# Decay attention feeding a mixture of attention experts: another written order of the same steps

## The chip, the cores and the metric

The kernel runs on one core of one Trainium2 chip. The metric is the device time of one execution in microseconds. One execution was also recorded by the hardware profiler; the rows shown below come from it. Engines carry the profile's names: PE is the matmul engine (TensorE), PEld its weight loads, DVE is VectorE, ACT is ScalarE, POOL is GpSimd, SP is SyncE, which here issues nearly all DMAs.

## The reference

Two parts. The first is a linear attention whose state decays (batch 4, 8 heads, 768 positions, 48 values per head, so 384 per position). The second is, per batch, a causal softmax attention by each of four experts of width 64, projected to 384, of which the best two per position are mixed by a gate.

```python
for t in range(S):                                    # decay attention
    cur = einsum('bhd,bhe->bhde', u * k[t], v[t])
    y[t] = einsum('bhd,bhde->bhe', r[t], state + cur)
    state = w[..., None] * state + einsum('bhd,bhe->bhde', k[t], v[t])
x = y.transpose(0, 2, 1, 3).reshape(B, S, 384)
logits = x @ w_gate                                   # mixture
topk, w = best two experts per position, softmax of their logits
for e in range(4):
    q, k, v = x @ wq[e], x @ wk[e], x @ wv[e]
    a = softmax(causal(q @ k.T / sqrt(64)))
    out += (weight of e per position) * (a @ v @ wo[e])
```

## The kernel before

The work is cut into 24 chunks of 128 positions (six per batch) and, for the mixture, into eight groups of three chunks (two per batch). A step of the first part is named by its chunk, such as `a_out,7`; one of the second by group, expert or pair of experts, and tile, such as `m_turn,7,3,5`.

First part, per chunk n: `load_chunk` and `load_vh` bring k, r and v. `a_decay` multiplies k and r by tables of powers of w (by DVE for the first three chunks, which read the tables in PSUM, by POOL for the rest, which read the copies that `table_out` makes by ACT). `a_transpose` turns k and r on PE, with ACT copies. `a_scores` (L565) are the products within the chunk, `a_mask` (L571) their masking. `a_state` (L602), `a_sum` (L613, L618) and `a_put` (L623) carry the state on. `a_out` (L582) is 32 matmuls that give the chunk's output. The part with u goes another way: `a_ku` (L522, L524, POOL) multiplies k, r and u, and `a_own` (DVE) sums that per head (L534) into eight columns of the bank in which a_out puts its 384, and multiplies v by the sums (L536). `a_add` (L586, DVE) adds that to a_out's columns. `a_xt` (L630) turns the sum on PE, with a copy by ACT (L633) and the rest by DVE in `a_xl` (L640).

Second part: `m_proj` (L670) gives queries and keys, as high and low parts (L680 and L682, or L685, L687 and a DMA). `m_values` (L705) gives values and gate logits, which DVE (L708) and ACT (L710) take out of one bank, `m_gate` the weights. `m_scores` (L753, L754) go to DVE for the maximum (L760) and ACT for the exponential (L762). `m_weigh` has DVE form factors (L768, L769) and POOL apply them (L775). `m_turn` (L783) transposes on PE and copies by ACT (L787), `m_av` (L803) multiplies by the values, with copies to high (L810, ACT) and low parts (L812, DVE), and `m_out` (L826 to L828) projects, copies (L835, ACT) and stores (L840).

All matmul outputs live in four PSUM buffers `ps` of one bank each and two `psb` of two banks each. The last av step, `m_av,7,1,3,6`, goes by thirds: matmuls of one third, high copy, then low copy and the matmuls of the next third, all in one bank. `m_out,7,2`, the last tile of the output, is made and stored in two halves.

No scheduler orders the work. `ORDER` lists 1724 words. Each advances one step to its next yield, and that emits instructions on the queue of each engine, which runs them in the order emitted. What stands behind a slash are buffer numbers for what the step takes. Semaphores between engines come from the framework: it orders accesses to the same data, and any two engines' accesses to one PSUM bank, by the order in which they are emitted.

```python
    for word in ORDER.split():
        word, _, spots[:] = word.partition("/")
        name, *args = word.split(",")
        key = (name, *(int(x) for x in args))
        if key not in under_way:
            under_way[key] = steps[name](*key[1:])
        if under_way[key] is None or next(under_way[key], done) is done:
            done.add(key)
```

Of the kernel before, what the change touches and what calls it, by code (L numbers as in the profile page):

```python
# [21 lines left out]
load_chunk,2 a_state,0/1 a_transpose,0 a_decay,1,1 a_transpose,1/2 a_transpose,1 a_sum,0 a_decay,2,0 a_ku,0/0 a_ku,0  # L22
a_own,0/30 a_sum,0/1 a_state,1/1 a_scores,0/0 a_sum,1 pad,3 a_scores,1/2 a_mask,0 a_mask,1 a_decay,2,1 a_transpose,2/1
a_put,0 load_zv,2 copy_vh,2 a_transpose,2/1 load_zv,2 a_put,1 a_out,0 a_add,0 a_state,2/0 a_ku,1/0 a_decay,3,0
make_sums,1 a_sum,1/0 a_sum,2 a_transpose,2/1 a_xt,0/2 a_out,1/3 load_chunk,4 load_qk,0/4 load_chunk,3 load_vh,3
load_o,0/5 load_chunk,5 a_ku,1 load_chunk,4 load_qk,2/0 load_qk,1/1 a_own,1/0 a_add,1 a_clear,0 a_decay,3,1 a_ku,2/0
a_sum,2/1 make_lower make_sums,0 a_ku,2 a_decay,4,0 a_decay,4,1 a_transpose,2 a_scores,2/0 a_xt,0/0 hi_qk,0 a_put,2
a_transpose,3/1 a_transpose,3/0 a_xl,0/0 a_transpose,3/3 a_xt,1/2 copy_vh,3 make_lower a_xt,1 a_transpose,3 a_mask,2
a_out,2/1 a_state,3/0 a_own,2/0 a_add,2 a_xt,2/1 a_transpose,4/3 hi_qk,2 a_xl,1 a_sum,3 lo_qk,0 a_xt,2 a_scores,3/2
hi_o,0 hi_qk,1 a_transpose,4/1 load_zv,3 a_transpose,4/0 a_transpose,4 a_xl,2 lo_qk,1 lo_qk,2 m_proj,0,0,0/1  # L30
m_proj,0,0,0/0 a_put,3 a_clear,2 a_clear,1 a_ku,3/0 a_ku,3 load_chunk,5 a_decay,5,1 a_decay,5,0 load_vh,4 load_v,1/2
load_v,0/3 load_vh,5 load_chunk,6 a_decay,6,0 a_sum,3/0 m_proj,0,1,0/3 m_proj,0,1,1/0 a_mask,3 lo_o,0 hi_v,0 load_zv,3
hi_v,1 a_own,3/20 m_proj,0,0,0 a_out,3 lo_v,0 m_proj,0,1,1/0 m_proj,0,1,1 m_proj,0,1,1 m_proj,0,1,1 a_add,3 copy_vh,4
a_scores,4/1 a_state,4/0 a_ku,4/0 load_o,1/4 load_v,2/1 a_ku,4 m_proj,0,1,0 m_proj,0,1,0 m_proj,0,1,0 m_proj,0,1,0
hi_v,2 lo_v,1 lo_v,2 load_zv,5 hi_o,1 a_sum,4 m_proj,0,0,1/2 load_zv,5 m_proj,0,0,1/1 m_proj,0,0,0/01 load_chunk,6
a_sum,4/1 a_decay,6,1 m_scores,0,0,2/1 m_values,0,0/3 m_scores,0,0,2/00 m_proj,0,0,1 m_values,0,0/0 a_mask,4 load_zv,4
# [15 lines left out]
m_proj,1,1,0 m_proj,1,1,0 m_proj,1,1,0 a_own,6/00 a_transpose,7 a_out,6 m_scores,0,3,2/52 m_proj,1,1,1 m_proj,1,1,1
m_scores,0,3,0/33 a_add,6 a_state,7/3 a_scores,7/1 m_weigh,0,2/2 a_sum,7 a_mask,7 m_scores,0,3,1 m_scores,0,3,0
m_proj,1,1,1 m_scores,0,3,2 m_weigh,0,3/3 m_proj,1,1,1 a_ku,7/0 a_ku,7 m_weigh,0,2 load_vh,8 m_proj,1,0,0/45 a_sum,7/0
m_weigh,0,3 m_scores,1,0,1/0 m_proj,1,0,1/0 m_proj,1,0,1/1 m_turn,0,2,0/3 m_turn,0,2,0/6 m_values,1,2/1 m_turn,0,2,1/2
m_turn,0,2,1/7 m_proj,1,0,1 m_scores,1,0,1/01 m_turn,0,2,2/3 m_turn,0,2,2/8 a_xt,6/0 a_xt,6/0 a_xl,6/0 m_values,1,2
# [5 lines left out]
load_zv,8 a_state,8/3 a_sum,8 a_decay,10,1 a_ku,8/0 a_sum,8/1 a_clear,6 a_ku,8 a_decay,10,0 a_scores,8/2
m_proj,1,0,1/01 m_av,0,0,0,3/1 a_state,9/0 a_mask,8 a_sum,9 m_scores,1,0,2 a_put,8 m_gate,1/111 m_weigh,1,0/0
a_transpose,9/3 a_transpose,9/0 m_av,0,0,0,3/0 m_av,0,0,0,3/0 a_transpose,9/2 a_xt,7/0 m_scores,1,1,1/0 a_transpose,9
m_av,0,1,0,3/3 m_scores,1,1,2 m_av,0,1,0,3/1 a_xt,7 a_out,8/1 m_weigh,1,0 m_av,7,1,0,3 a_own,8/0 m_av,0,1,0,3/1 a_xl,7
a_add,8 m_scores,1,2,2/1 m_turn,1,0,4/2 m_turn,1,0,4/0 m_turn,1,0,3/3 m_turn,1,0,3/4 m_scores,1,1,0 m_turn,1,0,0/0
m_turn,1,0,1/1 m_turn,1,0,2/2 m_turn,1,0,1/1 m_turn,1,0,0/3 m_out,0,2/3 m_scores,1,1,1/52 m_scores,1,2,2/00
load_chunk,11 m_out,0,2/0 a_ku,9/0 a_ku,9 load_vh,11 load_zv,11 load_vh,11 load_chunk,12 load_chunk,13 load_chunk,12
load_vh,10 load_vh,10 load_chunk,11 m_scores,1,2,1/0 a_xt,8/1 a_xt,8 a_transpose,10/0 m_scores,1,1,1 a_transpose,10/1
a_put,9 a_xl,8 a_scores,9/3 m_proj,2,0,0/1 m_scores,1,2,0/1 m_turn,1,0,5/0 m_turn,1,0,2/2 m_turn,1,0,5/5  # L70
m_proj,2,0,0/0 a_transpose,10/2 a_transpose,10 m_scores,1,2,2 m_scores,1,2,1/41 a_mask,9 a_own,9/30 m_weigh,1,1/1
m_weigh,1,1 a_sum,9/0 a_clear,8 a_ku,10/0 a_decay,11,0 a_decay,12,0 a_decay,11,1 a_out,9 a_state,10/0
m_scores,1,2,0/15 m_proj,2,0,0 a_add,9 a_sum,10 m_proj,2,1,0/1 m_turn,1,1,1/2 m_turn,1,1,1/6 m_proj,2,1,0/2
m_turn,1,1,3/3 m_scores,1,3,2/0 m_turn,1,1,4/0 m_proj,2,1,0 m_turn,1,1,4/a m_proj,2,1,0 m_proj,2,1,0 a_put,10
m_out,0,0/2 m_out,0,0/1 m_turn,1,1,3/7 m_proj,2,0,1/0 m_turn,1,1,2/1 m_scores,1,2,1 m_turn,1,1,2/9 m_turn,1,1,0/2
# [813 lines left out]
```

## Time and profile before

| | us |
|---|---|
| median of 3 runs (lowest, highest) | 371.22 (371.04, 371.96) |
| the profiled execution, its own time | 371.7 |
| its span, first to last instruction | 370.0 |
| PE busy | 337.8 |
| ACT, DVE, POOL busy | 261.1, 234.6, 195.8 |
| mean granted PE clock | 0.986 |

Busy times are the union of an engine's instructions. The number in brackets at the end of a timeline row is the idle time of the engine ahead of that row, and the instruction whose end released it. The releaser is inferred: a wait for several semaphores is put down to the one that came last, so where the engine named had been done for long, another was meant. A row with a count (x32) merges instructions that follow each other.

### The profile page before, as it was taken

How to read it: one execution, taken by the hardware profiler on the slowest of the kernel's cores; microseconds unless marked ns; L12 is line 12 of the kernel's file. 1: busy time of each engine (PE TensorE's matmuls, PEld its weight loads, DVE VectorE, ACT ScalarE, POOL GpSimd, SP SyncE). 2: the span in 40 equal slices, each digit the busy share in tenths (PEclk: the TensorE clock that was granted, in tenths of full speed). 3: DMA queues.
4: the chain of work that ended last, by engine and by line, in shares of the span. 5: the costliest groups of instructions: out<-in, count | busy, mean ns of one | idle time of the engine just before them, and what ended most of it. 6: DMA issues, size and time to landing. Idle time of an engine off the chain costs nothing.

```text
span 370.0 us, 10112 instructions
## 1 busy us (share of the span) xinstructions
PE 337.8 (91%) x3806; PEld 297.8 (81%) x3806; DVE 234.6 (63%) x648; ACT 261.1 (71%) x648; POOL 195.8 (53%) x272
## 2 busy tenths in 40 slices
...
GB/s 131 135 163 153 122 178 119 65 94 174 50 155 79 149 99 61 102 143 73 203 130 71 163 150 62 23 173 96 35 196 52 104 122 3 0 194 66 21 44 64
DMA packets 118628, 39.01 MB, mean 105 GB/s; under 512 B 111026, under 2 KB 114484, under 8 KB 118580
## 3 DMA queue, kind: packets, MB, share of 16 engines
...
q8 instruction: 30, 0.49, 0.6%
...
## 4 chain that ended last, share of the span: by engine, by line
PE 54%; DVE 10%; ACT 7%; DMA 5%; SPq 3%; issue 3%; POOL 2%; DVEq 0%; ACTq 0%; POOLq 0%
PE ps L670 8%; PE ps L783 8%; PE ps L803 8%; PE ps L582 5%; PE ps L705 4%; PE psb L753 4%; PE psb L754 4%; PE ps L546 3%; PE ps L565 2%; PE ps L602 2%; DVE tk L682 2%; PE ps L826 2%; DMA rdbuf<-in_r_dram 2%; PE ps L828 2%; PE ps L827 2%
## 5 line engine op out<-in xcount | busy, mean ns | idle before, releaser
L775 POOL TENSOR_SCALAR pr<-pr,f,gate 128x128 f32<-128x128 f32 (+5 forms) x96 | 67.5, 716 | 94.8 <-DVE f L769 41.7
L787 ACT ACTIVATE pt<-ps 128x384 f32<-128x384 f32 (+2 forms) x143 | 55.2, 419 | 33.3 <-PE ps L783 32.3
L760 DVE CUSTOM_DVE_ANT_0 pr<-psb,after 128x256 f32<-128x256 f32 (+5 forms) x96 | 58.5, 619 | 22.2 <-PE ps L783 11.5
L762 ACT ACTIVATE pr<-pr,nm 128x384 f32<-128x384 f32 (+5 forms) x96 | 63.8, 666 | 7.3 <-DVE nm L760 6.5
L783 PE MATMUL ps<-ident,pr 128*128 128x128 f32 x336 | 54.9, 278 | 2.7 <-DVE ownv L586 1.3
L753 PE MATMUL psb<-tk,tq 128*128 128x384 f32 (+2 forms) x144 | 49.5, 346 | 0.3 <-DVE nm L760 0.3
L783 PEld LDWEIGHTS ps<-ident,pr 128*128 128x128 f32 x336 | 39.0, 140 | 8.3 <-ACT pt L787 2.2
L754 PE MATMUL psb<-tk,tq 128*128 128x384 f32 (+2 forms) x144 | 42.2, 311 | 0.0
L803 PE MATMUL ps<-pt,vv 128*64 128x384 f32 (+2 forms) x322 | 40.7, 391 | 1.6 <-DVE yl L812 1.6
L571 DVE TENSOR_TENSOR rabuf<-ps,before 64x512 f32<-64x512 f32 x48 | 33.1, 689 | 6.6 <-PE ps L565 5.7
L582 PEld LDWEIGHTS ps<-zvbuf,rabuf 128*64 128x64 f32 x768 | 25.9, 141 | 14.0 <-ACT rabuf L557 4.2
L582 PE MATMUL ps<-zvbuf,rabuf 128*64 128x48 f32 x768 | 28.2, 227 | 9.7 <-DVE ownv L536 5.3
L670 PE MATMUL ps<-xt_hi,wqk_hi 128*128 128x384 f32 x96 | 33.9, 353 | 1.0 <-DVE xt_lo L640 0.4
L803 PEld LDWEIGHTS ps<-pt,vv 128*64 128x64 f32 x322 | 21.2, 137 | 16.8 <-issue 10.6
L670 PE MATMUL ps<-xt_hi,wqk_lo 128*128 128x384 f32 x96 | 32.4, 338 | 0.6 <-DVE wqk_lo L479 0.6
L522 POOL TENSOR_TENSOR ku<-kdbuf,uw 128x384 f32<-128x384 f32 x24 | 24.1, 1006 | 15.8 <-DVE ps L534 13.8
L670 PE MATMUL ps<-xt_lo,wqk_hi 128*128 128x384 f32 x96 | 32.3, 336 | 0.0
L557 ACT ACTIVATE rabuf<-ps 64x512 f32<-64x512 f32 x48 | 28.3, 590 | 4.1 <-PE ps L546 3.6
L753 PEld LDWEIGHTS psb<-tk,tq 128*128 128x128 f32 x144 | 27.3, 190 | 1.9 <-issue 0.7
L623 ACT ACTIVATE zvbuf<-z 64x384 f32<-64x384 f32 x48 | 24.9, 519 | 4.8 <-DVE z L613 4.3
L565 PE MATMUL ps<-rabuf,kt 128*64 128x64 f32 x768 | 27.0, 223 | 1.1 <-DVE ownv L586 1.1
L515 POOL TENSOR_TENSOR rdbuf<-rdbuf,tab_r 128x384 f32<-128x384 f32 x21 | 21.8, 1041 | 11.0 <-DMA rdbuf<-in_r_dram 11.0
...
## 6 DMA issues: line engine op xcount, KB each, us to landing
...
```

The source lines that it names most:

```text
L565: nc.tensor.matmul(ps[rows, i, p, :], kt[:, p, half], ra[:, par, i, p, :], start=True, stop=True)
L571: nc.vector.tensor_tensor(ra[rows, par].rearrange("s i p t -> s (i p) t"), ps[rows].rearrange("s i p t -> s (i p) t"), before[rows, None, ...
L582: nc.tensor.matmul(ps[half, 2 * p + par, :], ra[:, par, i, p, :], zv[:, par, i, p, :], start=True, stop=True)
L670: nc.tensor.matmul(ps, a[:, t, m0:m0 + P], x[:, t, :], start=i == 0, stop=i == n - 1)
L753: nc.tensor.matmul(o, tq[:, 0, q], tk[:, e, :n], start=True, stop=False)
L754: nc.tensor.matmul(o, tq[:, 1, q], tk[:, e, :n], start=False, stop=True)
L760: nc.vector.tensor_tensor_reduce(pr[:, :N], ps, after[:, S - N:], 1.0, 3e38, op0=OP.add, op1=OP.min, accum_out=nm)
L762: nc.scalar.activation(pr[:, :N], pr[:, :N], AF.Exp, bias=nm, scale=-1.0, accum_out=sums[:, e, j, 0:1])
L775: nc.gpsimd.tensor_scalar(p[:, :N], p[:, :N], f[:, i], gate[:, i, e:e + 1], op0=OP.mult, op1=OP.mult)
L783: nc.tensor.transpose(pst[:, j, :], mg[G]["p", e, j][:, i * C:(i + 1) * C], ident)
L787: nc.scalar.activation(pt[:, j0:], pst[:, j0:], AF.Copy)
L803: nc.tensor.matmul(psy[par * HD:par * HD + HD, j0 * C:j1 * C], vv[:, i % GC, e, :], mg[G]["t", e, i][:, j0:j1].rearrange("s j t -> s (j t) ...
```

## The change

The text of `ORDER` is replaced as a whole: another order of the same 1724 steps, each as often as before, with other buffer numbers. No step's code, no size and no buffer count changes. In the new text, accesses of two engines to one bank were counted as kept in order of issue when the order was laid out. Of some 400 lines these are the first and last ones of both orders and some with the steps of chunks 5, 7, 16, 17 and 21:

```diff
@@ -14,209 +14,210 @@
 PSUM = bass.MemoryType.PSUM
 
 ORDER = """
-load_vh,1 pad,6 warm_up/0 warm_up/0 make_after load_w pad,1 make_before zero,0 clear_vh,2 zero,2 zero,1 load_w pad,5
-powers/1 pad,0 pad,4 table,0/2 copy_vh,1 load_zv,1 load_zv,1 table,1/3 pad,2 powers load_vh,0 load_chunk,0 load_zv,0
-copy_vh,0 load_uw load_chunk,1 load_chunk,0 load_chunk,1 a_sum,0/0 clear_vh,1 make_ones make_ident clear_vh,0 load_uw
-table,0/0 table,1 load_zv,0 load_uw/1 table_out,1 table_out,0 load_uw a_decay,0,0 a_decay,1,0 a_decay,0,1
-a_transpose,1/2 a_transpose,0/3 a_transpose,1/0 a_transpose,0/1 a_transpose,0/0 load_chunk,2 load_chunk,3 load_vh,2
...
-m_scores,0,1,0/54 a_mask,5 m_weigh,0,0/0 m_scores,0,1,0 a_clear,3 load_vh,7 m_weigh,0,0 a_own,5/10 a_out,5 a_add,5
...
-a_transpose,8/1 m_scores,1,1,0/0 a_transpose,8/2 m_scores,1,1,0/23 a_own,7/00 m_gate,1 a_transpose,8 m_scores,1,0,0
-m_turn,0,3,2/b a_out,7 m_scores,1,1,2/34 a_add,7 load_vh,9 load_zv,9 load_vh,9 load_vh,8 load_chunk,10 load_zv,8
...
-m_turn,3,3,1/6 m_turn,3,3,0/a m_scores,4,0,2/21 a_xt,16 m_scores,4,1,1/1 m_turn,3,3,4/1 m_turn,3,3,4/8 a_out,17/0
-a_state,18/1 m_scores,4,1,0/0 a_transpose,18 m_turn,3,3,5/2 a_own,17/0 a_add,17 a_xl,16 a_xt,17/0 m_scores,4,1,2
...
-m_scores,7,3,1/50 m_scores,7,3,0/02 m_out,6,0/1 m_scores,7,3,2 m_turn,7,2,0/3 m_turn,7,2,4/2 m_turn,7,2,4/9 m_out,6,0
-m_out,6,2/0 m_av,7,0,0,3/2 m_scores,7,3,1 m_scores,7,3,0 m_weigh,7,3/3 m_weigh,7,3 m_turn,7,1,4/2 m_out,6,2/1
-m_turn,7,2,0/3 m_out,6,2 m_out,6,1 m_turn,7,2,5/1 m_turn,7,2,5/1 m_turn,7,2,1/0 m_turn,7,2,3/3 m_turn,7,2,2/1
-m_av,7,0,3,6 m_turn,7,2,2/a m_turn,7,2,1/0 m_turn,7,2,3/8 m_turn,7,3,1/1 m_turn,7,3,0/0 m_turn,7,3,2/3 m_turn,7,3,1/4
-m_turn,7,3,0/b m_turn,7,3,2/2 m_turn,7,3,3/1 m_turn,7,3,3/5 m_av,7,1,3,6/0 m_turn,7,3,4/3 m_turn,7,3,5/1
-m_turn,7,3,4/6 m_av,7,1,3,6/0 m_av,7,0,3,6/1 m_turn,7,3,5/0 m_av,7,1,3,6/0 m_av,7,1,3,6 m_av,7,1,3,6 m_av,7,0,3,6/1
-m_av,7,1,3,6 m_out,7,0/3 m_out,7,0/1 m_out,7,0 a_sum,11 m_av,7,1,3,6 m_out,7,2/1 m_out,7,2/0 m_out,7,2/2 m_out,7,2/0
-m_out,7,2 m_out,7,1/0 m_out,7,1/0 m_out,7,1 a_sum,5
+load_w clear_vh,1 make_ident clear_vh,0 load_w make_ones make_after zero,1 zero,2 zero,0 a_sum,0/0 make_sums,0
+load_vh,1 pad,4 pad,3 pad,1 pad,5 pad,6 pad,0 warm_up/0 warm_up/0 load_uw load_uw load_uw/1 load_chunk,0 load_vh,0
+load_zv,1 load_zv,1 copy_vh,1 load_uw copy_vh,0 load_zv,0 load_chunk,1 load_chunk,0 powers/1 powers pad,2 table,0/2
+table,1/3 table,0/0 table,1 a_decay,0,0 a_decay,1,0 a_state,0/2 a_transpose,0/3 a_decay,0,1 a_sum,0 load_chunk,1
+a_decay,1,1 a_transpose,1/0 load_zv,0 table_out,0 a_transpose,0/0 a_transpose,1/1 a_ku,0/0 a_ku,0 load_chunk,2
+load_qk,1/4 load_chunk,2 load_vh,2 a_transpose,0/1 load_chunk,3 a_transpose,0 a_sum,0/1 make_before clear_vh,2
...
+m_scores,0,1,1/55 a_transpose,6/2 a_own,5/30 a_transpose,6/0 m_scores,0,2,2/1 a_transpose,6/0 m_scores,0,2,0/0
+m_turn,0,0,0/2 a_out,5 a_sum,6 m_scores,0,2,0/03 a_add,5 load_chunk,8 a_ku,6/0 a_decay,8,0 a_sum,6/1 a_ku,6
...
+m_av,3,0,3,6/0 a_own,16/10 a_out,16 m_weigh,3,3/3 a_sum,17 m_weigh,3,3 m_proj,4,0,0/45 m_av,3,0,3,6/0 a_sum,18
...
+a_put,18 m_scores,4,1,2 m_scores,4,1,1/32 m_weigh,4,0/0 a_xl,16 m_gate,4/000 m_av,3,1,0,3/3 a_out,17/1 m_av,3,1,3,6
+a_scores,18/2 m_scores,4,1,1 a_transpose,19/1 m_av,3,1,3,6/1 a_own,17/0 m_weigh,4,0 m_weigh,4,1/1 a_add,17
...
+a_own,21/00 a_out,21 m_weigh,5,1/1 m_proj,6,1,0 m_av,4,1,0,3/3 m_proj,6,1,0 a_add,21 m_proj,6,1,1 m_proj,6,1,0
...
+m_turn,7,2,5/0 m_turn,7,2,5/4 m_turn,7,2,3/1 m_turn,7,2,1/2 m_turn,7,2,0/0 m_turn,7,2,0/9 m_turn,7,2,1/3
+m_turn,7,2,3/7 m_weigh,7,3/3 m_weigh,7,3 m_av,7,0,3,6 m_av,7,0,3,6/0 m_av,7,0,3,6/1 m_turn,7,3,0/0 m_turn,7,3,1/2
+m_turn,7,2,2/1 m_turn,7,3,0/6 m_turn,7,3,1/8 m_turn,7,2,2/0 m_turn,7,3,2/0 m_turn,7,3,2/1 m_turn,7,3,3/3
+m_turn,7,3,3/5 m_av,7,1,3,6/2 m_turn,7,2,4/1 m_turn,7,3,4/0 m_turn,7,3,5/3 m_av,7,1,3,6/1 m_turn,7,3,5/0
+m_turn,7,2,4/a m_turn,7,3,4/2 m_av,7,1,3,6/0 m_out,7,0/3 m_av,7,1,3,6 m_av,7,1,3,6 m_out,7,0/0 m_av,7,1,3,6 m_out,7,0
+m_out,7,1/1 m_out,7,1/1 m_out,7,1 m_av,7,1,3,6 m_out,7,2/0 m_out,7,2/0 m_out,7,2/3 m_out,7,2/0 m_out,7,2
 """
 
 BUFS = {
```

More of the change, by code (lines that the diff above doesn't have):

```diff
@@ L22 @@
[L22 to L36, printed above, removed]
@@ L52 @@
[L52 to L56, printed above, removed]
@@ L62 @@
[L62 to L75, printed above, removed]
-m_turn,1,1,0/8 m_values,2,0/3 m_scores,1,3,1/1 m_scores,1,3,2/33 m_scores,1,3,1/22 m_values,2,0/0 m_values,2,0/2
@@ new lines @@
+m_proj,1,0,0/0 m_scores,0,2,0 load_vh,7 load_chunk,7 load_chunk,8 load_zv,6 load_zv,6 load_zv,7 load_chunk,9 load_vh,7
+a_own,6/10 m_weigh,0,1 m_turn,0,1,0/3 m_turn,0,1,0/3 a_out,6 m_weigh,0,2/2 a_clear,4 a_decay,7,1 a_decay,8,1
+m_proj,1,0,0 a_clear,6 a_ku,7/0 a_ku,7 a_decay,9,0 m_weigh,0,2 a_state,7/0 load_vh,8 load_zv,7 load_vh,9
+m_proj,1,0,0/45 a_transpose,7/3 m_proj,1,1,1/1 m_proj,1,1,1 m_scores,0,3,0/32 m_proj,1,1,1 m_scores,0,3,0
+a_transpose,7 a_add,6 m_scores,0,3,1/1 m_proj,1,1,0/1 a_sum,7 m_proj,1,1,0 m_proj,1,1,1 m_values,1,2/0 m_values,1,2
@@ new lines @@
+a_put,8 a_mask,8 m_turn,0,3,2/3 a_xt,7/2 a_transpose,9/1 m_turn,0,3,2/b a_transpose,9/1 m_scores,1,1,0/1
+m_scores,1,0,1 a_transpose,9/3 m_av,0,1,0,3/0 a_transpose,9 m_av,0,1,0,3/1 a_xt,7 a_own,8/10 m_scores,1,1,1/45
+m_scores,1,1,0/54 m_av,0,1,0,3/1 m_weigh,1,0/0 a_out,8 a_add,8 a_xl,7 a_scores,9/3 a_state,9/0 a_sum,8/1 a_sum,9
+a_mask,9 m_scores,1,1,1 m_scores,1,1,0 a_ku,9/0 load_chunk,12 load_zv,10 load_chunk,13 load_vh,10 load_vh,10
+load_chunk,11 m_weigh,1,1/1 m_out,0,1/1 m_values,2,1/2 m_out,0,1/0 m_values,2,1/0 a_decay,10,0 m_weigh,1,0 a_xt,8/0
@@ new lines @@
+m_proj,2,1,0/2 m_scores,1,2,2 m_out,0,0/0 a_own,9/00 a_state,10/2 a_out,9 m_scores,1,3,1/43 m_proj,2,1,0
+m_scores,1,3,0/52 a_add,9 a_sum,10 a_scores,10/3 m_scores,1,3,1 m_gate,2 m_proj,2,1,0 m_proj,2,1,0 m_scores,1,3,0
+a_put,10 a_mask,10 a_scores,11/0 a_mask,11 m_proj,2,1,1/2 m_proj,2,1,1 m_proj,2,1,1 a_decay,12,0 a_decay,13,0 a_xt,9/1
+a_xt,9/1 a_decay,12,1 a_ku,10/0 a_ku,10 a_sum,10/1 a_sum,12/0 a_transpose,12/3 a_transpose,12/0 m_proj,2,0,0/23
+load_zv,12 load_vh,12 m_av,1,0,0,3/0 m_scores,1,3,2 a_xl,9/1 m_weigh,1,2/2 m_weigh,1,2 a_own,10/30 m_weigh,1,3/3
@@ new lines @@
+m_weigh,1,3 m_av,1,0,3,6 a_state,11/1 a_sum,11 m_av,1,0,3,6/0 m_proj,2,1,1 a_out,10 load_chunk,13 load_vh,12
+m_proj,2,0,1/45 m_out,0,0 m_out,0,2 a_ku,11/0 a_ku,11 m_proj,2,1,1 a_put,11 a_add,10 m_av,1,0,3,6/0 a_state,12/1
+a_sum,12 load_vh,13 load_chunk,14 load_vh,13 load_zv,12 m_turn,1,2,5/2 m_turn,1,2,5/5 m_turn,1,2,3/3 m_scores,2,0,0/1
+m_turn,1,2,3/9 m_turn,1,2,1/0 m_turn,1,2,4/2 m_turn,1,2,4/0 m_turn,1,3,5/1 m_turn,1,2,1/6 m_turn,1,3,5/1
+m_scores,2,0,2/0 m_turn,1,2,2/3 m_turn,1,2,2/4 m_turn,1,2,0/2 m_turn,1,2,0/3 m_turn,1,3,0/0 m_turn,1,3,3/1
@@ new lines @@
+a_add,11 a_xl,10 a_decay,14,0 a_clear,9 a_decay,13,1 a_ku,12/0 m_weigh,2,0 a_scores,12/2 m_turn,2,0,0/3 a_xt,11/0
+m_scores,2,2,2/1 m_turn,2,0,0/3 a_xt,11 m_out,1,0/1 m_turn,2,0,1/3 m_turn,2,0,1/8 m_scores,2,1,2 m_out,1,0/0
+m_scores,2,1,1 a_ku,12 a_clear,11 a_sum,13/0 a_clear,10 a_mask,12 a_xl,11 m_scores,2,1,0/34 m_scores,2,1,0
+a_transpose,13/2 m_proj,3,0,0/0 m_proj,3,1,0/3 m_proj,3,0,0/1 a_transpose,13 m_scores,2,2,2/20 a_own,12/10
+m_proj,3,1,0/0 m_scores,2,3,2/0 m_scores,2,2,0/1 a_out,12 m_proj,3,0,0 m_weigh,2,1/1 m_proj,3,1,0 m_proj,3,1,0
@@ new lines @@
+m_proj,3,1,1 m_scores,2,3,1/1 a_state,14/0 a_sum,14 m_scores,2,2,2 m_scores,2,2,0 m_scores,2,2,1 a_out,13
+a_scores,14/0 m_proj,3,1,1 a_add,13 m_proj,3,0,1 a_mask,14 a_put,14 m_out,1,2/2 a_decay,15,0 a_decay,16,0
+m_values,3,0/1 a_transpose,15/3 m_turn,2,1,2/0 m_weigh,2,2/2 m_values,3,0/1 m_out,1,2/1 m_values,3,0/0
+m_scores,2,3,0/0 a_transpose,15/1 m_turn,2,1,2/4 m_values,3,2/2 a_ku,14/0 load_chunk,16 a_decay,16,1 a_decay,15,1
+a_clear,13 a_transpose,16/1 a_transpose,16/0 load_chunk,18 m_proj,3,0,0/01 load_vh,16 load_vh,15 load_zv,15 load_vh,16
@@ new lines @@
+m_scores,3,1,2 m_scores,3,1,1/55 m_values,4,2/3 m_turn,3,0,1/2 m_turn,3,0,0/6 m_proj,4,1,0 m_values,4,2/0
+m_scores,3,1,0/33 m_scores,3,1,1 m_values,4,2/1 m_av,7,1,0,3 m_scores,3,1,0 a_scores,15/1 a_scores,16/0 m_av,2,1,0,3/3
+a_mask,15 m_turn,3,0,1/7 m_av,2,1,0,3/1 m_weigh,3,1/1 a_mask,16 m_av,2,1,0,3/1 load_zv,15 m_proj,3,0,1/23 load_zv,16
+load_chunk,17 a_ku,15/0 a_ku,15 a_decay,18,0 m_weigh,3,1 load_chunk,18 a_decay,18,1 a_sum,16/1 m_out,1,2 load_vh,17
+a_out,15/1 a_own,15/0 a_add,15 a_ku,16/0 a_decay,17,1 m_turn,3,0,5/2 m_out,2,2/0 m_turn,3,1,2/3 m_scores,3,2,0/0
```

301 lines of the change are left out of this document (151 added, 150 removed).

## The prediction

> **What bounds the kernel now.** I read the page first, then the waits of the matmul engine, then single places in the timeline. The profiled execution took 371.7 us for a span of 370.0 us; the median of the runs is 371.22 us, 0.48 us less. From the page (engine totals, then the chain that ended last):
>
> ```profile
> span 370.0 us, 10112 instructions
> ...
> PE 337.8 (91%) x3806; PEld 297.8 (81%) x3806; DVE 234.6 (63%) x648; ACT 261.1 (71%) x648; POOL 195.8 (53%) x272
> ...
> PE 54%; DVE 10%; ACT 7%; DMA 5%; SPq 3%; issue 3%; POOL 2%; DVEq 0%; ACTq 0%; POOLq 0%
> ```
>
> PE is busy for 337.8 of 370.0 us, so 32.2 us are idle. No other engine is above 71%. A new order adds and removes no instruction, so what it can change is these 32.2 us, plus stretches at a lower clock. Who ends PE's idle time (waits of PE: us in total, times, longest), and how long ScalarE waits for PE in one step:
>
> ```profile
> PE ps L582 <- DVE ownv L536: 5.3, 6, 2.0
> PE ps L630 <- DVE ownv L586: 2.8, 3, 1.3
> PE ps L582 <- ACT tk L680: 1.8, 2, 1.0
> PE ps L582 <- ACT rabuf L557: 1.7, 2, 1.5
> PE ps L546 <- DVE ownv L586: 1.6, 2, 1.3
> PE ps L803 <- DVE yl L812: 1.6, 2, 0.9
> PE ps L783 <- DVE ownv L586: 1.3, 1, 1.3
> PE ps L565 <- DVE ownv L586: 1.1, 1, 1.1
> PE ps L582 <- ACT pt L787: 0.3, 1, 0.3
> ...
> ACT pt L787 <- PE ps L783: 32.3, 34, 3.2
> ```
>
> The four L582 rows make 5.3 + 1.8 + 1.7 + 0.3 = 9.1 us. L582 is a_out. It needs nothing that a_own (L534, L536) computes: the two touch different columns of one bank, and only a_add (L586) needs both. Two of these waits in the timeline, chunks 5 and 7:
>
> ```profile
> 60.60 0.56 DVE L536 TENSOR_TENSOR ownv<-vhbuf,ps 128x384 f32<-128x384 f32 x1
> 61.30 1.95 PE L582 MATMUL ps<-zvbuf,rabuf 128*64 128x48 f32 x32 [2.02 <-DVE ownv L536]
> ...
> 88.25 0.55 DVE L536 TENSOR_TENSOR ownv<-vhbuf,ps 128x384 f32<-128x384 f32 x1
> 88.91 1.14 PE L582 MATMUL ps<-zvbuf,rabuf 128*64 128x48 f32 x32 [1.55 <-ACT rabuf L557]
> ```
>
> a_own ends at 61.16 and 88.80, PE starts 0.14 and 0.11 us later. So the second wait too is for a_own, though a long finished ScalarE copy is named. One bank is kept in the order of the written list, whichever columns are meant.
>
> The rest of the waits on L586 is the reverse case, a_own written behind a_out (chunk 17):
>
> ```profile
> 225.69 1.14 PE L582 MATMUL ps<-zvbuf,rabuf 128*64 128x48 f32 x32
> ...
> 226.97 0.56 DVE L534 TENSOR_REDUCE ps<-ku 128x8 f32<-128x384 f32 x1 [1.39 <-PE ps L582]
> 227.57 0.55 DVE L536 TENSOR_TENSOR ownv<-vhbuf,ps 128x384 f32<-128x384 f32 x1
> 228.16 0.56 DVE L586 TENSOR_TENSOR ownv<-ps,ownv 128x384 f32<-128x384 f32 x1
> ...
> 228.77 0.55 PE L630 MATMUL ps<-ident,ownv 128*128 128x128 f32 x3 [0.76 <-DVE ownv L586]
> ```
>
> From the end of a_out (226.83) to the next matmul that needs its sum or its bank are 1.94 us, all on VectorE. What PE has to do meanwhile is what the order decides.
>
> **The change, term by term.** Durations of PE steps, from the chain of waits (start, us):
>
> ```profile
> 75.09 1.14 PE ps L582 x32
> 76.23 0.68 PE ps L602 x16
> 76.91 0.93 PE ps L565 x32
> 78.62 1.55 PE ps L670 x9
> ...
> 113.02 0.66 PE ps L783 x6
> ```
>
> (1) a_own ahead of a_out. In the order before, 12 chunks (3, 5, 6, 7, 9, 11, 13, 14, 15, 16, 21, 23) have no PE step written between the two; PE waited in all but chunk 21, 9.1 / 11 = 0.83 us each. In the new order there are 6 such chunks (4, 8, 14, 16, 19, 21). What remains: if VectorE begins a_own as PE begins the step ahead, PE waits for 1.25 us (1.11 of a_own and 0.14) less that step. Those steps take 1.05, 0.64, 0.47, 0.68, 0.47 and 1.55 us (by the durations above; scores and value products in proportion to their columns), which leaves 0.2 + 0.6 + 0.8 + 0.6 + 0.8 + 0 = 3.0 us. The same sum over the twelve of before gives 6.5 us, where 9.1 were measured, so I raise it by 9.1 / 6.5 to 4.1 us. Gain 5.0 us. Ends: 2.5 us if all six cost 0.83 and four chunks with only 0.33 to 0.55 us between (3, 6, 7, 12) cost 0.4 each; 9.1 us if none waits.
>
> (2) a_own behind a_out: 7 chunks in both orders. PE work from the end of a_out to the next step that needs the sum or the bank, summed with the durations above: before 1.37, 0.68, 1.56, 1.32, 0.92, 0.93, 1.32 us (chunks 1, 2, 8, 10, 17, 18, 20), against the 1.94 short by 5.5 in all. New: 2.38, 1.56, 1.95, 2.13, 1.57, 3.21, 2.32 (chunks 1, 2, 15, 17, 20, 22, 23), short by 0.8. The rows on L586 hold 2.8 + 1.6 + 1.3 + 1.1 = 6.8 us, part of it where VectorE was late for other reasons. I take 4.0 us (2.0 to 6.0).
>
> (3) The end. Per third of the last output, the next matmuls into the bank wait for the copies of the third before:
>
> ```profile
> 359.34 1.31 PE L803 MATMUL ps<-pt,vv 128*64 128x128 f32 x20 [0.86 <-DVE yl L812]
> 361.38 1.42 PE L803 MATMUL ps<-pt,vv 128*64 128x128 f32 x21 [0.73 <-DVE yl L812]
> ...
> 366.57 0.49 ACT L835 ACTIVATE o<-ps 128x384 f32<-128x384 f32 x1 [1.40 <-PE ps L828]
> ...
> 367.09 0.33 SPq L840 DMA_DIRECT2D out_dram<-o  x1
> ```
>
> Ahead of the first of these waits three transposes stand as cover (3 x 0.11 us), ahead of the second nothing. New: five transposes (0.55 us) and m_out,7,0, six matmuls at 1.55 / 9 = 0.17 us, 1.03 us. So the first wait falls by 0.22 us and the second goes: 1.0 us (0.2 to 1.6). The last output is now a half, not a whole, so the copy of 0.49 us gets shorter; the store behind it stays about 2.6 us (367.42 to 370.0).
>
> (4) The start. The first decay reads the bank of tables behind ScalarE's two copies of it:
>
> ```profile
> 7.04 1.10 PE L434 MATMUL psb<-ident,pr 128*128 128x128 f32 x8 [1.21 <-DVE pr L428]
> ...
> 8.76 0.47 ACT L438 ACTIVATE tab_r<-psb 128x384 f32<-128x384 f32 x1
> 9.13 0.47 ACT L438 ACTIVATE tab_k<-psb 128x384 f32<-128x384 f32 x1
> ...
> 9.63 1.02 DVE L513 TENSOR_TENSOR kdbuf<-kdbuf,psb 128x384 f32<-128x384 f32 x2 [2.04 <-ACT tab_k L438]
> ```
>
> In the new list the decays of chunks 0 and 1 are written ahead of both copies, so they could start at 8.2, not 9.6. Against that, the loads of the rows w and u, which followed the first load of k, now go ahead of it. I take 1.0 us (-0.5 to 1.4; negative if the loads of the first chunks, issued in another order, come later).
>
> (5) The clock. Windows (us, PE, weight loads, DVE, ACT, POOL busy, then the granted clock):
>
> ```profile
> 57.50:61.00 3.50, 1.33 (x9) 1.06 (x9) 3.33 (x10) 2.74 (x6) 1.72 (x4) 1.00 0.97 183
> 61.00:64.50 3.50, 3.20 (x49) 3.01 (x49) 1.18 (x3) 1.33 (x5) 1.94 (x4) 0.51 0.69 119
> ```
>
> A stretch with PE busy for 1.33 of 3.5 us, holding two of the stalls above (a_out of chunk 5 among them), is followed by one at 0.51: 3.2 us of matmuls at half speed, 1.6 us lost. In the new order chunk 5 has 1.24 us of PE work between a_own and a_out. I take half, 0.8 us (-1.6 to 1.6), as the fall can come at another place. The Trainium skill ("TensorE: Matmul & The Clock Gate", What's actually happening) has the clock fall after at least one idle window of some 3.4 us. By that alone 2.02 us of idle would not have cost the clock and nothing would be won or lost here, and the forecast would be 0.8 x 0.7 = 0.6 us higher; the trace shows that a part-busy stretch suffices, and decides.
>
> Sum: 5.0 + 4.0 + 1.0 + 1.0 + 0.8 = 11.8 us. Not all arrives: PE comes sooner to steps whose inputs come from others. In the chain 10 + 7 + 5 + 3 + 3 + 2 = 30% of the span is not PE's, so as an estimate 30% of the gain, 3.5 us, turns into waits for loads, VectorE or GpSimd. That leaves 8.3: 371.7 - 8.3 = 363.4 us in the profile's terms, less 0.48 for the median: **362.9 us**. The ends of the terms, with the same 30%, are 2.9 us (2.5 + 2.0 + 0.2 - 0.5 and the clock as now, 4.2) and 13.8 us (9.1 + 6.0 + 1.6 + 1.4 + 1.6, 19.7). That most of it arrives is supported by the ScalarE row, 32.3 us of waiting for PE's transposes: the engines behind PE have room.
>
> **Rivals.**
> - *All of it arrives.* Nothing is given back: 371.2 - 11.8 = 359.4 us. For it: ScalarE and VectorE wait for PE. Against: the 30%.
> - *The a_out waits stay.* 17 chunks still have a_own ahead of a_out, as before. If the wait follows from that and not from the place, term 1 is nothing: (11.8 - 5.0) x 0.7 = 4.8, so 366.4 us. Against: no stall in the five chunks that had PE work between.
> - *The clock falls more often.* Two more stretches like 61.0 to 64.5, and the old one kept: 362.9 + 0.8 + 3.2 = 366.9 us.
> - *Slower: VectorE blocked by GpSimd.* Now that a_out waits for a_own in the plan, a_own is written early, and behind it on VectorE queue score reductions, masks and sums, which free PE's banks. If it comes before a_ku is done, all of them wait for a GpSimd operation:
>
> ```profile
> POOL ku L522 <- DVE ps L534: 13.8, 8, 3.9
> ...
> L524 POOL TENSOR_TENSOR ku<-ku,rdbuf 128x384 f32<-128x384 f32 x24 | 24.6, 1025 | 0.8
> ```
>
> Half of one such operation in each of 24 chunks is 24 x 0.51 = 12.3 us: 375 us. It decides from 8.3 / 24 = 0.35 us a chunk. Against it: now GpSimd waits for VectorE (13.8 us), and only 4 chunks of the new order (3 before) have under 1.5 us of PE work between a_ku and a_own.
> - *No change.* The semaphores kept each bank in order before too; the new list meets other waits of the same size, 371 us.
>
> **How the numbers follow.** Forecast 0.40, all arrives 0.20, a_out waits stay 0.17, clock 0.08, blocked by GpSimd 0.09, no change 0.06. A measurement of this kernel can tell about 0.3% (1.1 us) from nothing. Faster: 0.40 + 0.20 + 0.17 + 0.08 = 0.85; same 0.06; slower 0.09. The range takes the first four: 357.0 (371.2 less the 13.8 of the best ends is 357.4) to 369.0 us (371.2 less the 2.9 of the worst ends is 368.3). The forecast's own range is 360 to 366.
>
> **What would show it.** In the profile after: the four a_out rows fall from 9.1 to about 4 us, those on L586 from 6.8 to under 3, L803 behind L812 from 1.6 to about 0.6, VectorE's wait for tab_k is gone, and there is no stretch near 0.5 after the first 20 us. PE's idle falls from 32 to about 24 us at the same busy time. Wrong if PE's idle stays above 30 us: then look at who ends it, loads and a_ku first.

## The result, and the profile after

The kernel after takes 345.37 us (345.03 to 346.38, four runs) against 371.13 us of the kernel before on the same chip: a ratio of 0.931 [0.928, 0.935], 25.8 us faster. Measured again later, it took 344.77 against 371.84 us, 0.929 [0.926, 0.933]. The forecast was 362.9 us, range 357.0 to 369.0: the sign was right, the gain three times as large as said.

The page of the kernel after, engine totals and the chain that ended last (its lines are numbered one higher than before: a_out is L583, a_own L535 and L537, a_add L587):

```profile
span 344.7 us, 10135 instructions
...
PE 332.6 (97%) x3806; PEld 297.4 (86%) x3806; DVE 232.8 (68%) x648; ACT 261.2 (76%) x648; POOL 194.8 (57%) x272
...
PE 83%; POOL 6%; DVE 4%; ACT 4%; issue 3%; POOLq 0%; ACTq 0%; DVEq 0%
```

PE's idle time is 344.7 - 332.6 = 12.1 us, where it was 32.2. PE has 83% of the chain (77% in another execution of the same kernel, e14 below) instead of 54%. The busy times of VectorE, ScalarE and GpSimd change by less than 2 us. Who still ends idle time of PE (us in total, times, longest):

```profile
PE ps L360 <- DVE pr L356: 2.1, 1, 2.1
PE ps L804 <- DVE rabuf L572: 1.7, 2, 1.5
PE ps L671 <- DVE wqk_lo L480: 1.1, 1, 1.1
...
PE ps L583 <- ACT xt_hi L634: 0.8, 1, 0.8
...
PE ps L583 <- DVE ownv L537: 0.2, 1, 0.2
```

The a_out rows, 9.1 us before, are 0.8 + 0.2 = 1.0 us. The 0.8 us is chunk 2, whose a_own stands behind its a_out; its wait before (0.5 us, for other causes) was not among the 9.1. So of the 9.1 us 0.2 are left, those of chunk 5. There is no row for the sum of a_add (6.8 us before) and none for the last thirds behind the low copy (1.6 us before). Chunks 6 and 8 in the timeline, to be held against those of chunks 5 and 7 before:

```profile
64.24 0.56 DVE L537 TENSOR_TENSOR ownv<-vhbuf,ps 128x384 f32<-128x384 f32 x1
65.22 1.14 PE L583 MATMUL ps<-zvbuf,rabuf 128*64 128x48 f32 x32
...
88.00 0.54 DVE L535 TENSOR_REDUCE ps<-ku 128x8 f32<-128x384 f32 x1
...
88.58 0.55 DVE L537 TENSOR_TENSOR ownv<-vhbuf,ps 128x384 f32<-128x384 f32 x1
...
89.48 1.09 PE L583 MATMUL ps<-zvbuf,rabuf 128*64 128x48 f32 x32
```

The multiply is the last operation of a_own. It ends 0.42 and 0.35 us ahead of a_out, and neither a_out row has a wait. Windows of the kernel after around the place where the clock fell before (us, PE, weight loads, DVE, ACT, POOL busy, granted clock):

```profile
57.00:61.00 4.00, 3.85 (x77) 3.39 (x78) 2.81 (x11) 3.58 (x8) 3.78 (x5) 1.00 0.69 117
61.00:64.00 3.00, 3.00 (x29) 2.93 (x26) 2.44 (x6) 2.38 (x9) 2.89 (x6) 1.00 0.56 100
```

PE is busy 3.85 of 4 us where it was busy for 1.33 of 3.5, and the clock stays at 1.00. (A 128x128 transpose is issued every 0.11 us there, as at full clock elsewhere, so the column can be trusted here; see the last section.)

Idle time alone does not add up to the gain: it fell by 20.1 us, the span by 25.3. The other 5.2 us are busy time that went. The stretch at half clock was 1.6 us of it. The rest is the end of the pipeline. All 768 matmuls of a_out in the kernel after, by their line (ns: shortest, median, longest):

```profile
L583 PE MATMUL ps<-zvbuf,rabuf x768: 206/222/258, 19.4 to 286.6; 128*64 128x48 f32 x192
```

One takes 222 ns, but in the row at 65.22 us 32 of them take 1.14 us, 36 ns each, because the next starts while the last is in the pipe. When nothing follows, the last 0.222 - 0.036 = 0.19 us of the matmul, its drain, still count as busy in the profile, though no new work begins. The starts of the matmuls show what the busy time hides. Take as the usual step the median distance from a matmul of one shape to the start of the next; a start that comes more than 0.25 us later than that is a stop. Before there are 44 stops with 34.4 us of lateness together, after 17 with 10.0 us. That is 24.4 us, the gain but for the clock, and 27 stops fewer are 27 x 0.19 = 5.1 us of drains. With the clock's 1.6 us this makes 6.7 us, more than the 5.2 us of busy time that went: in the profiled execution two early steps of PE took 1.97 and 1.64 us, where the kernel before took 1.10 and 0.91 us, which is 1.6 us the other way.

### The profile page after: what moved, and what is told of

Same layout as the page of the kernel before. It is cut to its first block, busy times and chain, and to the rows that moved or that the text cites. A ratio compares the mean times of both kernels' runs of the same rounds, so it can differ in the third digit from the quotient of the medians.

```text
span 344.7 us, 10135 instructions
## 1 busy us (share of the span) xinstructions
PE 332.6 (97%) x3806; PEld 297.4 (86%) x3806; DVE 232.8 (68%) x648; ACT 261.2 (76%) x648; POOL 194.8 (57%) x272
## 4 chain that ended last, share of the span: by engine, by line
PE 83%; POOL 6%; DVE 4%; ACT 4%; issue 3%; POOLq 0%; ACTq 0%; DVEq 0%
PE ps L784 11%; PE ps L804 11%; PE ps L671 10%; PE ps L706 8%; PE psb L755 6%; PE psb L754 6%; PE ps L547 6%; PE ps L583 6%; PE ps L566 5%; PE ps L603 5%; PE ps L827 3%; PE ps L829 2%; PE ps L828 2%; PE ps L631 2%; DVE rabuf L572 2%
## 5 line engine op out<-in xcount | busy, mean ns | idle before, releaser
L763 ACT ACTIVATE pr<-pr,nm 128x128 f32<-128x128 f32 (+5 forms) x96 | 63.9, 667 | 2.4 <-DVE nm L761 1.4
L784 PE MATMUL ps<-ident,pr 128*128 128x128 f32 x336 | 52.6, 276 | 0.1
L804 PE MATMUL ps<-pt,vv 128*64 128x384 f32 (+2 forms) x322 | 40.2, 392 | 1.7 <-DVE rabuf L572 1.7
L804 PEld LDWEIGHTS ps<-pt,vv 128*64 128x64 f32 x322 | 20.9, 137 | 18.1 <-issue 12.6
L671 PE MATMUL ps<-xt_lo,wqk_hi 128*128 128x384 f32 x96 | 32.2, 336 | 0.0
L754 PEld LDWEIGHTS psb<-tk,tq 128*128 128x128 f32 x144 | 27.3, 189 | 0.8 <-DVE nm L761 0.2
L583 PEld LDWEIGHTS ps<-zvbuf,rabuf 128*64 128x64 f32 x768 | 24.8, 138 | 3.5 <-issue 1.2
L583 PE MATMUL ps<-zvbuf,rabuf 128*64 128x48 f32 x768 | 26.8, 223 | 0.9 <-ACT xt_hi L634 0.8
L755 PEld LDWEIGHTS psb<-tk,tq 128*128 128x128 f32 x144 | 27.3, 190 | 0.0
L516 POOL TENSOR_TENSOR kdbuf<-kdbuf,tab_k 128x384 f32<-128x384 f32 x21 | 21.8, 1046 | 8.3 <-DMA kdbuf<-in_k_dram 7.4
```

The costliest lines, as they stand in the source:

```text
L583: nc.tensor.matmul(ps[half, 2 * p + par, :], ra[:, par, i, p, :], zv[:, par, i, p, :], start=True, stop=True)
L671: nc.tensor.matmul(ps, a[:, t, m0:m0 + P], x[:, t, :], start=i == 0, stop=i == n - 1)
L754: nc.tensor.matmul(o, tq[:, 0, q], tk[:, e, :n], start=True, stop=False)
L755: nc.tensor.matmul(o, tq[:, 1, q], tk[:, e, :n], start=False, stop=True)
L763: nc.scalar.activation(pr[:, :N], pr[:, :N], AF.Exp, bias=nm, scale=-1.0, accum_out=sums[:, e, j, 0:1])
L784: nc.tensor.transpose(pst[:, j, :], mg[G]["p", e, j][:, i * C:(i + 1) * C], ident)
```

## The experiments

Theory A, as the first expectations call it: the gain is that of the waits which come from one bank being kept in order (a_own and a_out above all). Theory B: those waits only uncover others, and the gain is the layout as a whole.

### Is it the shared bank?

e1 is the kernel before with the eight sums of a_own in a tile of SBUF instead of in the bank of a_out. No word of the order moves.

```diff
+    ownsum = const.tile([P, H], F32, name="ownsum")
     def a_own(n):
-        own = outs(n)[:, DM:DM + H, None]
+        outs(n)
+        own = ownsum[:, :, None]
```

> The order before, but a_own puts its eight sums of every chunk into an SBUF tile, so a_own and a_out share no PSUM bank and neither waits for the other; no word of the order is moved. Theory A (the gain is the waits that come from one bank being kept in order, and all of it arrives): 9.1 us on a_out and some 5.5 of the 6.8 us on a_add go, with them about 0.17 us of matmul drain at each of some 20 stalls (3 us) and the clock's fall at 61 us (1.6 us): 371 - 19 = 352 us. Theory B (the new layout is better as a whole; a wait that goes uncovers another, as in the prediction's 30% or more): 371 - 7 to 9 = 362 to 364 us.

Measured 358.08 against 372.04 us, 0.964 [0.961, 0.967]: 14.0 us, between the two theories. The a_out rows of PE's waits in e1 (L585 there):

```profile
PE ps L585 <- ACT kt L555: 0.9, 2, 0.7
PE ps L585 <- DVE yl L815: 0.6, 1, 0.6
PE ps L585 <- DVE rabuf L574: 0.3, 1, 0.3
```

None of these is for a_own. 0.5 us of the 1.8 are chunk 2's, which stood before too, so the 9.1 us became 1.3. The waits for the sum of a_add fell as well, from 6.8 to 3.0 us: where a_own is written behind a_out, it no longer waits for a_out to end. So 14.0 of the 25.8 us that the new order gains can be had, without moving a word, from the bank that a_own and a_out share.

e2 and e3 do the same for chunks 7, 11, 14 and for chunk 5 alone (`if n in (7, 11, 14): own = ownsum[:, :, None]`).

> The order before with the sums in SBUF for chunks 7, 11 and 14 only. Their a_out waited 1.55 + 1.53 + 0.90 = 3.98 us. Theory A: these and three drains of 0.17 us arrive whole, 4.5 us, 366.6 us. Theory B: at most 70% of 3.98, 2.8 us, 368.3 us or more.

> The order before with the sums in SBUF for chunk 5 only, whose a_out waited 2.02 us just ahead of the fall of the clock at 61 us. If the clock falls because of that stall: 2.0 + 0.2 + 1.6 = 3.8 us, 367.3 us, and the profile has no half-speed stretch after 20 us. If the stall alone counts: 2.2 us, 368.9 us, with the stretch still there.

e2: 369.58 us, 0.994 [0.992, 0.997], 2.5 us (1.3 to 3.0 by the interval) of the 4.0 that it could give. e3: 369.08 us, 0.993 [0.991, 0.995], 3.0 us (1.8 to 3.5), between its two cases. The windows of its profiled execution:

```profile
57.00:60.50 3.50, 2.21 (x28) 1.97 (x29) 3.33 (x11) 2.54 (x6) 1.67 (x5) 0.89 0.90 171
60.50:64.00 3.50, 3.50 (x45) 3.28 (x42) 2.38 (x5) 1.54 (x5) 2.87 (x5) 0.62 0.70 113
```

With the stall of chunk 5 gone PE is still busy for only 2.21 of 3.5 us there, and the clock still falls (0.62). But that is one execution. The mean granted clock of a whole execution is 0.999 or 1.000 in four of the seven of e3, which as far as the clock column tells leaves no room for such a stretch (3.4 us at half clock make it 0.995); the kernel before never has more than 0.995, here and in the later experiments. So the stall of chunk 5 had a part in the fall, and is not all of it. In e1, where the neighbouring stalls go too, 57 to 64 us run at 1.00.

e4 is the same edit in the kernel after.

> The new order with the sums of every chunk in SBUF. Its waits of PE behind a_own are 0.2 us by the profile (0.8 more under another name). Theories A and B both: 0 to 1.2 us faster, 344.2 to 345.4 us. If the new order gained nothing from where a_own stands, it would gain here what the order before gains in the first of these runs.

347.7 us, 0.936 [0.932, 0.940] of the kernel before: nothing gained, and some 2 us lost, though this interval overlaps that of the kernel after. In the new order the bank costs nothing that this experiment can see. The loss may be a side cost of the SBUF tile, which e1 would pay too (last section).

### Is it the place of a_own?

e7 is the kernel after with a_own of chunks 3 to 14 moved down to stand directly ahead of their a_out. For chunk 8 (words of `ORDER`, line breaks left out):

```diff
-a_own,8/10 m_scores,1,1,1/45 m_scores,1,1,0/54 m_av,0,1,0,3/1 m_weigh,1,0/0 a_out,8
+m_scores,1,1,1/45 m_scores,1,1,0/54 m_av,0,1,0,3/1 m_weigh,1,0/0 a_own,8/10 a_out,8
```

> The new order with the a_own words of chunks 3 to 14 moved down to just ahead of their a_out, as twelve chunks of the order before had it; nothing else moves. If the place of a_own ahead of a_out decides: seven of these lose 0.5 to 1 us of cover and PE waits about 0.8 us and a drain of 0.2 at each, 349 to 352 us, with rows of a_out behind a_own of 4 to 7 us. If the new layout absorbs it: 346 to 347 us.

359.48 us, 0.966 [0.959, 0.972] of the kernel before: 13 to 14 us of the 25.8 lost again by twelve words. Seven of the twelve a_out wait again (chunks 3, 4, 5, 8, 10, 13 and 14), 10.9 us in all, where 0.2 us were left. Chunk 8 in the timeline of e7:

```profile
90.03 0.81 DVE L761 CUSTOM_DVE_ANT_0 pr<-psb,after 128x640 f32<-128x640 f32 x1
90.16 1.52 PE L804 MATMUL ps<-pt,vv 128*64 128x384 f32 x12 [1.45 <-DVE rabuf L572]
90.77 0.68 DVE L761 CUSTOM_DVE_ANT_0 pr<-psb,after 128x512 f32<-128x512 f32 x1
...
92.24 0.56 DVE L813 TENSOR_TENSOR yl<-ps,yh 128x384 fp32r<-128x384 f32 x1 [0.79 <-ACT yh L811]
...
92.99 0.53 DVE L535 TENSOR_REDUCE ps<-ku 128x8 f32<-128x384 f32 x1
93.56 0.55 DVE L537 TENSOR_TENSOR ownv<-vhbuf,ps 128x384 f32<-128x384 f32 x1
94.21 1.14 PE L583 MATMUL ps<-zvbuf,rabuf 128*64 128x48 f32 x32 [2.54 <-ACT pr L763]
```

Chunk 8 is the clearest case, because a_own moved past no PE step: the PE step ahead of a_out (L804) is written ahead of both places of a_own. What changed is VectorE's queue: a_own now stands behind two score maxima, the low copy, which itself waits 0.79 us for ScalarE, and two small operations of m_weigh. In the kernel after a_own begins at 88.00 (shown above), ahead of all of them. PE stands 2.54 us for it (the ScalarE operation named had nothing to do with a_out). Here the price of a_own's place is set by what stands ahead of it on VectorE, at the same PE work. In other chunks of e7 words of PE were passed too, and the two are not separated.

e13 asks whether the place of a_own also holds the rest: a_own early in the order before, free of the bank, on top of e5 (below).

> As e5 (the order before, sums of a_own outside the bank, copies of one bank spaced, the new end; 354.9 us), and a_own of 17 chunks written earlier, to up to 3 us of PE work ahead of a_out where a_ku and the chunk before allow it. Theory 1, the place of a_own holds the rest too (a_add and what needs its sum no longer wait for a_own): 348 to 351 us, and the waits of PE for ownv (2.5 us in e5) gone. Theory 2, the rest is spread over the places of other steps: 353.5 to 355 us. If VectorE is blocked behind GpSimd's a_ku (the rival of the prediction): 357 us or more.

358.0 us, 0.964 [0.961, 0.967], 3 us longer than e5: theory 1 fell, and the time is that of the third case. Waits of PE and of VectorE in e13:

```profile
PE ps L632 <- DVE ownv L588: 2.7, 2, 2.2
...
DVE ownsum L536 <- POOL ku L524: 1.9, 1, 1.9
```

PE now waits longer for the sum of a_add, not less (1.4 us in e5), and once VectorE stands 1.9 us for GpSimd's a_ku: the rival "blocked by GpSimd", on a small scale. The longest wait has another cause, which the rows of VectorE and GpSimd ahead of it show:

```profile
283.71 1.00 POOL L522 TENSOR_TENSOR ku<-kdbuf,uw 128x384 f32<-128x384 f32 x1
283.72 1.06 DVE L723 TENSOR_TENSOR eq<-lg 128x48 f32<-128x48 f32 x1
...
284.79 1.00 POOL L524 TENSOR_TENSOR ku<-ku,rdbuf 128x384 f32<-128x384 f32 x1
284.81 1.04 DVE L724 TENSOR_TENSOR eq<-eq,lower 128x48 f32<-128x48 f32 x1
...
285.89 0.21 DVE L725 TENSOR_TENSOR gt<-gt,eq 128x48 f32<-128x48 f32 x1
```

In e5 this a_ku waited 1.35 us for a_own and began behind these gate operations. In e13 it meets them: two that run beside it take 1.06 and 1.04 us, the next, beside no a_ku, takes 0.21. (In e5 one of the two took 0.88 us, beside another operation of GpSimd.) a_add stands behind them.

### The other pairs on one bank, and the end

Several kinds of steps let ScalarE and VectorE read one bank in turn. e6 is the kernel before with two of them relieved: m_proj's two high copies first, then both low ones, and the gate logits read by ScalarE, which reads the values too. e5 is e1 with these and with the last words in the new order's sequence.

```diff
+            for e, own in ((2 * pr, top), (2 * pr + 1, bot)):
+                nc.scalar.activation(tk[own, e, :], ps[own], AF.Copy)
             for e, own, other in ((2 * pr, top, bot), (2 * pr + 1, bot, top)):
+                yield
                 if e % 2:
                     yield
-                nc.scalar.activation(tk[own, e, :], ps[own], AF.Copy)
-                yield
...
-        nc.vector.tensor_copy(logits_of(G)[:, j, :], ps[:, NV:])
+        nc.scalar.activation(logits_of(G)[:, j, :], ps[:, NV:], AF.Copy)
```

> The order before with only the two changes to m_proj (high key parts first) and m_values (logits by ScalarE); the sums stay in PSUM, the end as it was. ScalarE waited 7.9 us for VectorE's low key parts and 7.6 us behind VectorE's copy of the logits. Theory A: PE gets a good part of it, 364 to 367 us against 372. Theory B: PE does not notice, 370 to 372 us.

> The order before with the sums in SBUF (358.1 us alone), and two more one-bank pairs eased: m_proj has ScalarE make both high key parts before VectorE makes the low ones (one change of engine per key tile instead of three), m_values takes the gate logits by ScalarE (no VectorE read of that bank); and the last words as in the new order (m_out,7,0 and m_out,7,1 between the thirds of the last av step). The end alone: 0.86 + 0.73 and two drains, 1.9 us. Theory A (what is left of the gain, 12 us, are the other pairs of engines on one bank): 358.1 - 1.9 - 6 to 9 = 347 to 350 us. Theory B (what is left belongs to the layout as a whole): 354 to 356 us.

e6: 369.52 us, 0.993 [0.990, 0.995], 2.2 us. e5: 354.87 us, 0.955 [0.951, 0.958], 16.8 us, about 3 more than e1; 1.0 of them is the end (the last 200 matmuls begin 27.9 us ahead of the end of the span instead of 28.9; 27.1 in the kernel after). By the count of late starts e5 has 28 stops with 18.7 us, the kernel after 17 with 10.0 us: the 8.7 us between are about the 9 us between their times. They are not one place: transposes of k and r 2.7 against 1.7 us, of scores 3.6 against 0.5, a_out 2.9 against 1.2, a_xt 1.8 against 0.3, m_proj 2.0 against 1.2.

e8 was to price the spaced copies in the new order by putting them back to back.

> The new order with the four words of each key projection's copies, and the two of each value product's, written directly one behind the other, as most of them are in the order before. Theory A (spread pairs are a part of the gain): ScalarE's waits for VectorE on tk and vv rise from 3.6 and 2.6 us to about 8 each, and the time by 3 to 8 us, 349 to 354 us. Theory B: no more than 1 us, 345 to 347 us.

386.13 us, 1.038 [1.035, 1.042]. Moved so, a copy of group 7 overwrites a buffer of values before `m_av,5,1,0,3` has read it, so the end of this kernel computes something else than the reference, and its time prices nothing exactly. But that copy begins at 326 us at the earliest, and a_out of chunk 23 already starts at 320.9 us, 35 us later than in the kernel after (285.7). ScalarE's waits for VectorE's copy of the logits rise from 2.6 to 17.3 us, for the low key parts from 3.6 to 9.9. So the tight copies cost far more than the 3 to 8 us of theory A. How much of it is the spacing, and how much other work that stands behind copies written earlier, is not separated.

### The start

e12 is the kernel before with the two table copies written behind the first decays; e10 and e11 are the kernel after with a longer warm-up of PE.

Part of a line of `ORDER`:

```diff
-table,1 load_zv,0 load_uw/1 table_out,1 table_out,0 load_uw a_decay,0,0 a_decay,1,0 a_decay,0,1
+table,1 load_zv,0 load_uw/1 load_uw a_decay,0,0 a_decay,1,0 a_decay,0,1 table_out,1 table_out,0
```

> The kernel before, with only the two copies of the tables by ScalarE written behind the decays of chunks 0 and 1 instead of ahead of them. If these copies are what held the first decay (as the prediction's step 4 said), it starts at 8.3 instead of 9.6 us and 1.0 to 1.3 us arrive: about 370 us. If the clock then also stays at full through the first transposes, up to 3 us more. Rival: the loads or the other copies of ScalarE are next, nothing arrives: 371.2 us.

> The kernel after, with the warm-up matmuls 1 us earlier and 15 instead of 10 of them (first word of the list; they write a bank that is not used before 40 us). In the kernel after, transposes take 213 ns each from 8.1 us to 14.4 us and 109 ns afterwards, although the page shows 1.00 for all of it. If that is half clock because the ten warm-up matmuls began only at 2.1 us, the transposes of the tables take 0.9 us instead of 2.0, the first decay starts at 9.1 instead of 10.1, and 1 us arrives at the end: 344.4 us. Rival: the first chunks are bound by the loads and by the copies of ScalarE (which released the first state step at 10.7 us): no change, 345.4 us.

> As the one before, and six more warm-up matmuls behind the transposes of the tables, where PE is idle until 10.7 us. If the clock is kept at full from there on, what ran at half until 14.4 us (about 5.5 us of PE work between 10.7 and 15.7) takes half the time, and up to 2.7 us more arrive: 342 us; transposes of 109 ns from 8 us on. If the first chunks are bound by other engines, 344 to 345.4 us.

e12: 370.05 us, 0.996 [0.993, 0.999], about 1.5 us (0.6 to 2.7 by the interval). In its profiled execution the tables' transposes took 1.94 us instead of 1.10, and the decay began at 9.02 and not at 8.3 us. e10: 344.9 us, e11: 346.5 us, both within the intervals of the kernel after. In e11 the early work came sooner and PE then stood 2.2 us at one place for a mask of VectorE (1.5 us in the kernel after). Then e10's kernel again (e15) beside the kernel after itself (e14):

> The kernel after, unchanged, to stand beside the next one: 345.4 us.

> The kernel after with 15 warm-up matmuls from 1.25 us on, beside the kernel after in the same call. The profiles differ by 1.5 us in the span (343.2 against 344.7), the medians by 0.5 us. Theory: the transposes of the tables at full clock bring the first decay 0.6 us forward and that arrives: 344.8 us. Rival: no difference.

344.77 (e14) and 344.72 us (e15): no difference, so no version here beats the kernel after. The profile of e14, the same kernel as after, tells why. The tables' transposes and the first decay in the execution shown above, then in e14:

```profile
8.08 1.97 PE L435 MATMUL psb<-ident,pr 128*128 128x128 f32 x8
10.08 1.02 DVE L514 TENSOR_TENSOR kdbuf<-kdbuf,psb 128x384 f32<-128x384 f32 x2 [2.67 <-PE psb L435]
```

```profile
6.95 1.19 PE L435 MATMUL psb<-ident,pr 128*128 128x128 f32 x8 [0.19 <-DVE pr L429]
8.18 1.19 DVE L514 TENSOR_TENSOR kdbuf<-kdbuf,psb 128x384 f32<-128x384 f32 x2 [0.75 <-PE psb L435]
```

Eight transposes take 1.97 us in one execution and 1.19 in the other; the decay starts at 10.08 or 8.18 us, the span is 344.7 or 342.6 us. When full speed comes in the first 15 us differs between executions of one kernel, and the longer warm-up bought nothing in the median.

## Why the prediction was wrong, step by step

**What bounds it** held: PE's idle time was what a new order could change. That PE's busy time would stay was wrong by 5.2 us. A wait row leaves out the 0.19 us in which the last matmul drains: 5.1 us for the 27 stops that went, which no term of the sum had. In the profile's terms the forecast was 8.3 us, terms (1) to (5), 11.8, less 3.5 given back. Measured were 25.3 us: 8.9 on a_out, 6.8 on a_add, 1.6 at the end, 2.8 of PE's other waits and 5.2 of busy time.

**(1) a_own ahead of a_out**: forecast 5.0 of 9.1 us, measured 8.9. e1 shows the cause (the shared bank), so the mechanism was right and the size was off. The failed step is "if VectorE begins a_own as PE begins the step ahead": I let a_own begin 0.47 to 1.55 us ahead of a_out, the length of the PE step ahead. In all six chunks (4, 8, 14, 16, 19, 21) a_own began 1.5 to 2.0 us ahead of a_out and ended 0.35 to 0.86 us ahead of it, so none waits. The new list writes a_own ahead of other VectorE work there, and e7 shows for chunk 8 that this place decides. For chunk 8 the length was wrong too: its PE step (L804) was put at 0.64 us and takes 1.35 us to the start of a_out. That all six would go was the term's best end, and nothing in the prediction told it from the middle.

**(2) a_own behind a_out**: forecast 4.0, measured 6.8, all of the rows on a_add. The PE work counted behind a_out was enough. The allowance for "VectorE was late for other reasons" had a ground, as 3.0 us of these rows stay in e1, where a_own waits for no a_out; but the new order lifted those too, and which words did it is not shown.

**(3) The end**: forecast 1.0, measured 1.6 by the rows (1.8 by the last 200 matmuls). The first wait, of which I left 0.86 - 0.22 = 0.64 us, went too.

**(4) The start**: the forecast "could start at 8.2" was met to 0.02 us in e14 (8.18), and e12 gained about 1.5 us by this edit alone. In the profiled execution of the kernel after, transposes at half clock (1.97 us) put it off to 10.08.

**(5) The clock**: forecast 0.8, the half of 1.6 as a guess between its ends; measured 1.6, the half stretch is gone. The stall of chunk 5 was a part of the reason and not all of it: with it taken away (e3) the clock fell in the profiled execution and, by the mean clock, not in four of seven.

**The give-back of 30%** was the worst step. The runs show none. In e1 the a_out rows fell by 7.8, those of a_add by 3.8, the clock gave 1.6 and 15 stops fewer (44 to 29 by the count of late starts) 2.8 of drains, 16.0 us together; 14.0 arrived, and the edit may have a cost of its own of about 2 (e4). PE's other idle time, where a give-back would have to appear, is 32.2 - 9.1 - 6.8 = 16.3 us before and 20.9 - 1.3 - 3.0 = 16.6 in e1. In the new order it even fell, without the end's 1.6, from 14.7 to 12.1 - 0.2 = 11.9 us. Of the single stalls, e2 lost a part (2.5 of 4.0 us, within wide limits) and e3 nothing (3.0 us for a stall of 2.0). A share of the chain was no ground for the 30%: the chain before named only 84% of the span, and much of what was not PE's in it were the waits that were to go. In the kernel after 17% of the chain (23% in e14) is still not PE's.

**The rivals.** "All of it arrives" was right in that nothing is given back, and stopped 14 us short of the time. "The a_out waits stay" fell with the 0.2 us. "The clock falls more often" and "No change" did not come. "VectorE blocked by GpSimd" did not come either: no wait of a_own for a_ku is among the rows of the kernel after. e13 shows a wait of this kind (1.9 us, once) when a_own is written earlier still, and beside it a slower VectorE next to GpSimd; how the 3 us divide is not shown.

**What is shown and what is not.** Shown: the shared bank of a_own and a_out is worth 14 us in the order before (e1) and nothing in the new one (e4), and the place of a_own 13 to 14 us in the new one (e7). The other pairs on one bank together with the end give 3 more. The last 9 us are open. An earlier place of a_own does not bring them (e13, one such placing), a side cost of the SBUF tile of some 2 us may be a part, and by the count of late starts they lie spread over five kinds of PE steps. Which words bring them was not separated. Not tried: a_own early in the order before with the bank still shared, which would show what the place alone gives there.
